# A margin behind planned landings for prologue products, and another tie-breaking number, in a transformer block on one core

## The chip, the cores and the metric

The kernel runs on one core of one Trainium2 chip. The metric is the device time in microseconds of one execution, from runs of the same inputs; the profile is one further execution taken with the hardware profiler. Engines are named as in the profile: PE is TensorE, ACT is ScalarE, DVE is VectorE, POOL is GpSimd, SP is the engine that issues all DMAs here. A tile of tokens is 128 tokens; the sequence has 2048 tokens, so 16 tiles.

## The reference

Model width D = 1024, 32 heads of 32, feed-forward width F = 3584, everything in bf16. Two branches read the same normalised input and meet in a gate:

```python
def reference(A_x, A_wqkv, A_wo, B_x, B_w1, B_b1, B_w2, B_b2):
    def _A_ref(x, wqkv, wo):
        B, S, D = x.shape
        H = 32
        Dh = D // H
        qkv = (lambda x, *d: x.transpose(*d))((x @ wqkv).reshape(B, S, 3, H, Dh), 2, 0, 3, 1, 4)
        q, k, v = qkv[0], qkv[1], qkv[2]
        scores = jnp.einsum("bhqd,bhkd->bhqk", q, k) * (Dh ** -0.5)
        p = _softmax(scores, axis=-1)
        o = jnp.einsum("bhqk,bhkd->bhqd", p, v)
        return (lambda x, *d: x.transpose(*d))(o, 0, 2, 1, 3).reshape(B, S, D) @ wo
    def _B_ref(x, w1, b1, w2, b2):
        y = _layernorm(x, axis=-1)
        h = _gelu(jnp.einsum("bsd,df->bsf", y, w1) + b1)
        return jnp.einsum("bsf,fd->bsd", h, w2) + b2
    x = A_x
    xn = _layernorm(x, axis=-1)
    s = _A_ref(xn, A_wqkv, A_wo)
    g = _silu(_B_ref(xn, B_w1, B_b1, B_w2, B_b2))
    return x + s * g
```

The softmax takes 32 x 2048 x 2048 exponentials, and the kernel computes all of them on ACT.

## The kernel before

**An order made by a planner.** Every operation of the kernel is first recorded as a planned operation (`_Plan.add`) with an engine, a cost (`occ`), a latency and the operations it depends on. `_Plan.run` then plays the five engines forward in planned time and fixes, for each engine, the order in which its operations are issued. `settle` turns the dependencies into semaphore waits and `emit` writes the instructions. Only the order reaches the chip: a planned time is not kept, and each engine goes through its list in order and waits on semaphores.

**Work.** Heads are taken in 8 groups of 4 (`hg`), queries in 8 blocks of 256 (`qb`), keys in 8 blocks of 256 (`kp`). One unit (line 903) is one head group, one query block and one key block: PE makes the scores (8 matmuls, line 919), ACT takes two exponentials of 128x1024 each from PSUM (line 928), and later PE multiplies them with V (line 632). There are 512 such score groups and 1024 exponentials. DVE adds exponentials up for the softmax sums (lines 945, 959, 1329, 1332). The products of the feed-forward branch, the projections of Q, K and V for later head groups, and at the end the output projection, are "dense" work that fills PE between score groups.

**PE's choice.** `pe_step` (line 246) picks PE's next operation in planned time. Score groups come from `s_queue` in a fixed order and have precedence when they are ready or would be delayed (lines 256 and 349). Products of exponentials with V come from `pv_queue`. Dense work comes from named queues in `self.dense`: among them `pro` (the first K and Q blocks of head group 0), `q0` (its later Q blocks), `v0` (its V, in quarters of four tiles), `proj`, `mlp`, `w2`, `wo`. Only the head of each queue is a candidate, `next_dense` (line 219) sorts the heads by position, and an item that has begun is gone through to its end, with score groups between its matmuls. Dense and value items share two PSUM banks, 6 and 7. When PE has nothing to do for long, it may put in filler matmuls (line 329 on).

**The prologue.** Head group 0 can't start until tokens are normalised and turned, so that the model width lies across the partitions. Tiles 0 to 3 and 5 are turned on PE and evicted by ACT (line 804); tiles 4 and 6 to 15 are normalised by DVE into `gw` (line 816) and turned by a DMA from `gw` to `xnT` (line 820). The planner gives such a DMA 1300 ns on SP, 262144 bytes at 300 bytes per ns and for most tiles 1000 ns more (line 821). The products of the prologue read `xnT`: K block n (`k_item`, line 762) and Q block n (`q_item`, 752) tiles 2n and 2n+1, a Q pair of blocks (`qk_item`, 740) and a V quarter m (`v_half`, 726) tiles 4m to 4m+3. A V quarter has 32 matmuls, eight for each tile in order, evicted by DVE at line 736; a K block from the second on has 8 matmuls and is evicted at line 771, a Q block at 758, a Q pair at 748. An item becomes a candidate when its first matmul's operands are there in planned time; for a later tile of a V quarter nothing is asked.

In the score order (`order0`, line 1243) the scores that first need K block 5 are the 15th group, K block 6 the 17th, K block 7 the 19th.

**Tie-breaking numbers.** `nz` (line 83) makes a number between -1 and 1 from a seed, which belongs to a stretch of 30,000 ns of planned time (`plan.seeds`, `plan.seg`), and the operation's index. With seed 0 it is 0. It shifts the positions of `proj`, `mlp`, `w2` and `wo` items (by up to `amp` = 4, line 230), the priorities of DVE operations (by up to `jit` = 0.1, line 158) and the choice of the exponential after which an item of values may begin (line 272). Only the third stretch, 60 to 90 us of planned time, has a seed other than 0.

Of the kernel before, what the change touches and what calls it, by code (L numbers as in the profile page):

```python
# [32 lines left out]
class _Plan:  # L33
# [59 lines left out]
    def run(self):  # L93
# [86 lines left out]
        def bank_for():  # L180
            best = None
            for b in (6, 7):
                if owner[b] is not None and owner[b].k < len(owner[b].chunks):
                    continue
                r = 0.0
                for x in bank_free[b]:
                    if x.start is None:
                        break
                    r = max(r, x.fin)
                else:  # L190
                    if best is None or r < best[0]:
                        best = (r, b)
            return best
# [25 lines left out]
        def next_dense(t):  # L219
            out = []  # L220
            busy = any(owner[b] is not None and owner[b].mode == "v" and (owner[b].evacs[-1].fin or INF) > t for b in (6, 7))
            if not busy and S["pv"] < len(self.pv_queue):
                busy = self.pv_queue[S["pv"]].soon.start is not None
            for n in self.dense:
                q, h = self.dense[n], heads[n]
                if h < len(q) and q[h].hold <= S["s"]:
                    if q[h].due < S["s"] + self.lead:
                        out.append((q[h].due - 1e6, n, q[h]))
                        continue
                    amp = self.amp if n in ("proj", "mlp", "w2", "wo") else 0.0  # L230
                    out.append((q[h].pos - (self.w2b if n == "w2" and busy else 0.0) + amp * self.nz(t, q[h].chunks[0].idx), n, q[h]))
            out.sort(key=lambda x: x[0])
            return out
# [12 lines left out]
        def pe_step(t):  # L246
# [19 lines left out]
            if S["pvo"] is not None:  # L266
                it = S["pvo"]
                vo = it.chunks[it.k]
            elif S["pv"] < len(self.pv_queue):
                it = self.pv_queue[S["pv"]]  # L270
# [16 lines left out]
            if S["do"] is not None:  # L287
                it = S["do"]
                do = it.chunks[it.k]
                if do.left == 0:  # L290
                    d_at = do.ready
                else:
                    do = None
            else:
                bf = bank_for()
                for pos, n, it in next_dense(t):
                    o = it.chunks[0]
                    if it.need is not None and it.need.k < len(it.need.chunks):
                        continue
                    if o.left or (it.bank is None and (bf is None or (held and it.due >= S["s"] + self.lead))) or (it.evacs and not it.heirs and it.evacs[0].left > 1):  # L300
                        continue
                    if n == "w2" and not all(d.start is not None for c in it.chunks for d in c.deps if d.eng == "DVE"):
                        continue
                    if n == "wo" and not all(d.start is not None for d in it.chunks[-1].deps if d.eng != "PE"):
                        continue
                    r = o.ready if it.bank is not None else max(bf[0], o.ready)
                    if r < d_at:
                        do, dopen, d_at = o, (it, None if it.bank is not None else bf[1], n), r
                    if d_at <= t:
                        break  # L310
            v_ok, d_ok = v_at <= t, d_at <= t
            use = None
            it = dopen[0] if dopen else S["do"]
# [13 lines left out]
            if use is None:  # L327
# [5 lines left out]
                if bf is not None and bf[0] <= t and S["s"] < len(self.s_queue):  # L333
                    cw = 430.0 if t < 4800.0 else 220.0
                    wide = t < 4900.0 and nxt > t + cw + 200
                    n, w = (1, 4) if wide else (1, 1) if t < 6000.0 else (2, 1) if t < 10000.0 else (1, 2)
# [16 lines left out]
            if use == "v":  # L353
# [4 lines left out]
                it = S["pvo"]  # L358
# [3 lines left out]
            else:  # L362
# [5 lines left out]
                it = S["do"]  # L368
# [8 lines left out]
        while ev:  # L377
            t, ei = heapq.heappop(ev)
            e = ENGS[ei]
            if t < tf[e]:  # L380
                continue
            while ev and ev[0] == (t, ei):
                heapq.heappop(ev)
            if e == "PE":
                pe_step(t)
                continue
            o = pick(e, t)
            if o is not None:
                commit(o, t)
                if e == "ACT":  # L390
                    S["dry"] = tf[e]
                    for x in pend[e]:
                        if x.prio == 0:
                            S["dry"] += x.occ
                    for x in soon[e]:
                        if x[2].prio == 0:
                            S["dry"] += x[2].occ
            elif soon[e]:
                wake(max(t, soon[e][0][0]), e)
# [71 lines left out]
def bass_recurrent_scan__mha_block__mixer_channel_mlp__prompt_kernel(  # L471
# [24 lines left out]
    plan.pat1, plan.pat2, plan.guard = 3000.0, 900.0, 660.0  # L496
    add = plan.add
    plan.seeds = (
        0, 0, 235064808, 0, 0, 0, 0, 0, 0, 0, 0, 0, 0, 0, 0, 0, 0, 0, 0, 0, 0, 0, 0, 0, 0, 0, 0, 0, 0,
        0, 0, 0, 0, 0, 0, 0, 0)  # L500
    plan.seg, plan.amp, plan.jit = 30000, 4, 0.1

    with ExitStack() as st:
# [870 lines left out]
        for w in range(HG):  # L1374
            if 0 < w < HG - 1:
                proj(w + 1, w)
            if w == HG - 1:
# [6 lines left out]
                v0 = V[:, 1].rearrange("p t n -> p (t n)")  # L1384
# [14 lines left out]
            for qb in range(NQB):  # L1399
# [45 lines left out]
                for t2 in range(2):  # L1445
# [16 lines left out]
                    for nh in range(2):  # L1462
                        late = qb >= NQB - 2
                        fin = qb == NQB - 1
                        it = _Item("wo", 64 * 7 + 8 * qb + 4 * t2 + 2 * nh)
# [140 lines left out]
```

## Time and profile before

| what | value |
|---|---|
| median of 3 runs | 1027.97 us (1027.73 to 1028.23) |
| the profiled execution's own time | 1027.79 us |
| its span, first to last instruction | 1026.0 us |
| granted PE clock | 1.000 |
| exponentials of 128x1024 in PSUM | 1024, of which 988 into the P tiles by line 928: 918.9 us busy |
| DMA | 167.76 MB, mean 164 GB/s |
| tiles turned by DMA | 11, from issue to landing 2.7 / 2.9 / 4.4 us (least, median, most) |
| PE busy from 30 to 60 us | 27.74 of 30 us |
| PE busy from 60 to 90, from 90 to 120 us | 28.68, 29.95 of 30 us |

The table is read from the top: the profiled execution lies within the three runs, and 1.79 us of its time lie around the span. Times in views of the trace count from the span's first instruction. Busy time is the union of instruction times on an engine. In the timeline an instruction's start may lie a little inside the one before it, so the pace of a row of equal instructions is read from the starts of two pieces, not from the durations.

### The profile page before, as it was taken

How to read it: one execution, taken by the hardware profiler on the slowest of the kernel's cores; microseconds unless marked ns; L12 is line 12 of the kernel's file. 1: busy time of each engine (PE TensorE's matmuls, PEld its weight loads, DVE VectorE, ACT ScalarE, POOL GpSimd, SP SyncE). 2: the span in 40 equal slices, each digit the busy share in tenths (PEclk: the TensorE clock that was granted, in tenths of full speed). 3: DMA queues.
4: the chain of work that ended last, by engine and by line, in shares of the span. 5: the costliest groups of instructions: out<-in, count | busy, mean ns of one | idle time of the engine just before them, and what ended most of it. 6: DMA issues, size and time to landing. Idle time of an engine off the chain costs nothing.

```text
span 1026.0 us, 31917 instructions
## 1 busy us (share of the span) xinstructions
PE 993.4 (97%) x14227; PEld 632.5 (62%) x14294; DVE 953.4 (93%) x1364; ACT 1015.5 (99%) x1080; POOL 15.1 (1%) x23
## 2 busy tenths in 40 slices
PE   8899999999999999999999999999999999999997
PEld 6556665776666566656665676666666656564444
DVE  8999999999999998998999999998999889978987
ACT  8999999999999999999999999999999999999997
POOL 2200000000000000000000000000000000000000
PEclk9999999999999999999999999999999999999999
DMA  8558842766675767446456676566457753783331
GB/s 232 123 140 224 215 130 72 200 186 177 177 199 139 200 172 194 138 109 180 131 158 176 172 219 172 141 185 173 119 146 189 213 153 97 245 250 114 124 94 64
DMA packets 315761, 167.76 MB, mean 164 GB/s; under 512 B 54248, under 2 KB 303592, under 8 KB 315624
## 3 DMA queue, kind: packets, MB, share of 16 engines
q1 hardware_dynamic: 315624, 165.72, 57.8%
q8 instruction: 112, 1.84, 0.7%
q14 instruction: 25, 0.20, 0.1%
HBM read 146.55 MB, written 12.06 MB: 155 GB/s over the span
## 4 chain that ended last, share of the span: by engine, by line
ACT 92%; DVE 4%; PE 2%; DMA 1%; issue 0%; POOL 0%; SPq 0%
ACT P L928 84%; ACT ut L1146 5%; ACT P L1277 1%; PE ps L637 1%; ACT ut L1177 1%; DVE stats L856 1%; DMA xnT<-gw 1%; DVE PA L945 1%; DVE PR L959 1%; ACT w2r L928 1%; DVE gw L816 1%; DMA hT<-in_A_x_dram 0%; ACT gw L1177 0%; PE ps L919 0%; POOL lnp L865 0%
## 5 line engine op out<-in xcount | busy, mean ns | idle before, releaser
L928 ACT ACTIVATE P<-ps 128x1024 bf16<-128x1024 f32 x988 | 918.9, 1242 | 0.7 <-PE ps L919 0.7
L945 DVE TENSOR_TENSOR PA<-P 128x2048 bf16<-128x2048 bf16 x173 | 210.0, 1216 | 27.8 <-ACT P L928 27.3
L637 PE MATMUL ps<-yT,w1r 128*128 128x256 bf16 x1792 | 227.1, 273 | 1.1 <-DVE QKT L748 0.7
L637 PE MATMUL ps<-w2r,hT 128*128 128x256 bf16 x1792 | 222.9, 273 | 1.8 <-DVE V L722 1.1
L919 PE MATMUL ps<-QKT 32*128 32x256 bf16 x4032 | 200.2, 273 | 14.2 <-ACT P L928 11.4
L959 DVE TENSOR_TENSOR PR<-PR,PA 128x2048 bf16<-128x2048 bf16 x173 | 209.2, 1212 | 1.3
L637 PEld LDWEIGHTS ps<-yT,w1r 128*128 128x128 bf16 x1792 | 163.9, 98 | 53.4 <-issue 27.7
L637 PEld LDWEIGHTS ps<-w2r,hT 128*128 128x128 bf16 x1792 | 163.2, 98 | 51.4 <-issue 30.6
L919 PEld LDWEIGHTS ps<-QKT 32*128 32x128 bf16 x4032 | 59.8, 92 | 140.5 <-ACT P L928 135.4
L632 PE MATMUL ps<-P,V 128*32 128x256 bf16 (+1 forms) x4080 | 137.4, 272 | 0.0
L637 PE MATMUL ps<-xnT,wqk 128*128 128x512 bf16 (+2 forms) x534 | 119.3, 352 | 4.4 <-DMA xnT<-gw 1.0
L632 PEld LDWEIGHTS ps<-P,V 128*32 128x32 bf16 x4080 | 95.5, 96 | 32.3 <-issue 23.2
L637 PE MATMUL ps<-wv,xnT 128*128 128x256 bf16 (+2 forms) x704 | 87.4, 264 | 1.4 <-DMA xnT<-gw 1.4
L637 PEld LDWEIGHTS ps<-xnT,wqk 128*128 128x128 bf16 x584 | 49.5, 98 | 52.4 <-issue 15.8
L1115 DVE TENSOR_TENSOR hT<-ps,b1T 128x512 bf16<-128x512 f32 x112 | 76.7, 685 | 3.1 <-PE ps L637 2.5
L945 DVE TENSOR_TENSOR PR<-P 128x2048 bf16<-128x2048 bf16 x60 | 72.9, 1215 | 0.5 <-ACT P L928 0.5
L637 PEld LDWEIGHTS ps<-wv,xnT 128*128 128x128 bf16 x704 | 56.1, 98 | 22.9 <-issue 9.9
L1146 ACT ACTIVATE ut<-ut 128x3072 bf16<-128x3072 bf16 (+2 forms) x27 | 59.5, 2206 | 0.0
L748 DVE CAST QKT<-ps 128x512 bf16<-128x512 f32 x58 | 39.6, 683 | 1.5 <-PE ps L637 1.1
L1014 DVE STREAM_TRANSPOSE nt<-ps 128x256 f32<-128x256 f32 x63 | 28.0, 444 | 11.7 <-PE ps L632 11.5
L1140 DVE TENSOR_TENSOR ut<-hT 128x2048 bf16<-128x2048 bf16 (+1 forms) x37 | 35.2, 956 | 0.1
L1149 DVE TENSOR_TENSOR hT<-ut,hT 128x2048 bf16<-128x2048 bf16 (+1 forms) x37 | 35.1, 954 | 0.0
(121 smaller groups left out, 576.5 us busy)
## 6 DMA issues: line engine op xcount, KB each, us to landing
w1r<-in_B_w_dram SPq DMA_DIRECT2D x112, 512.0 KB, 4.3
w2r<-in_B_w_dram SPq DMA_DIRECT2D x128, 256.0 KB, 3.8
w2r<-in_B_w_dram SPq DMA_DIRECT2D x128, 192.0 KB, 3.7
yst<-in_A_x_dram SPq DMA_DIRECT2D x18, 256.0 KB, 4.6
wqk<-in_A_wqkv_dram SPq DMA_DIRECT2D x16, 256.0 KB, 3.5
g_scratch<-gw SPq DMA_DIRECT2D x32, 128.0 KB, 3.2
hT<-in_A_x_dram SPq DMA_DIRECT2D x14, 256.0 KB, 3.8
o_scratch<-ot SPq DMA_DIRECT2D x56, 64.0 KB, 3.2
```

Of the source, the lines that this page charges most:

```text
L632: ins = e.matmul(dst(j), lhsT=lhsT(j), rhs=rhs(j), start=start, stop=stop, tile_position=(0, 32 * j), skip_group_check=True)
L637: return e.matmul(dst, lhsT=lhsT, rhs=rhs, start=start, stop=stop, skip_group_check=True)
L748: dve(lambda e: e.tensor_copy(QKT[sl][:, which, tq * 512:(tq + 1) * 512], bank(it.bank)), c_ps(512), [], [(nm, sl, 2 * tq), (nm, sl, 2 * t ...
L919: ins = e.matmul(bank(b0[j], kk * 256, (kk + 1) * 256), lhsT=QKT[sl][32 * j:32 * j + 32, 1, kb * 128:(kb + 1) * 128], rhs=QKT[sl][32 * j:3 ...
L928: x = act(lambda e, h=h: e.activation(Pt[pi][:, 2 * h:2 * h + 2].rearrange("p j k q -> p (j k q)"), ps[:, pr[h] * 1024:(pr[h] + 1) * 1024] ...
L945: return dve(lambda e: e.tensor_tensor(dst[:].rearrange("p u j q -> p (u j) q"), src[:].rearrange("p u j k q -> p (u j) k q")[:, :, 0, :], ...
L959: return dve(lambda e: e.tensor_tensor(fl3(pr), fl3(pr), fl3(PA[i]), op=ALU.add), c_b16(2048), [("PA", i), tok], [tok], 3.2)
L1014: dve(lambda e: e.transpose(nt_t[:], bank(pv.bank, 256, 512)), c_ps(256) + 120, [], [("nt",)], prio, pv)
L1115: w1_ev[p] = dve(lambda e: e.tensor_tensor(hT[:, hs], bank(it.bank).rearrange("p (k t) -> p k t", k=2), b1T[:, 2 * pi:2 * pi + 2].unsqueez ...
L1140: dve(lambda e, u_=u_, x_=x_: e.tensor_tensor(u_, x_, x_, op=ALU.mult), c_b16(n), hs_, [("ut", ui)], gp)
L1146: act(lambda e: e.activation(ua, ua, ACT.Tanh, scale=GC), c_acts(run * 512), uts, uts, ga)
L1149: dve(lambda e, u_=u_, x_=x_: e.tensor_tensor(x_, u_, x_, op=ALU.mult), c_b16(n), [("ut", ui)] + hs_, hs_, gp)
```

## The change

A new condition in `pe_step`'s search for dense work: after 30 us of planned time, an item of `pro`, `q0` or `v0` is passed over as long as any of its matmuls reads something that a DMA brings which either has not been planned yet or whose planned landing plus 1600 ns lies later than the matmul's own place, taken as now plus 55 ns for each matmul ahead of it in the item. (Both branches of the written choice by position are 1600.) The seed of the third stretch is another number. Nothing else differs; the costs that the planner reckons with are the same.

```diff
                     if o.left or (it.bank is None and (bf is None or (held and it.due >= S["s"] + self.lead))) or (it.evacs and not it.heirs and it.evacs[0].left > 1):
+                        continue
+                    if n in ("pro", "q0", "v0") and t > 30e3 and any(d.eng == "SP" and (d.start is None or d.fin + (1600.0 if it.pos < 0.2 else 1600.0) > t + 55.0 * i)
+                                         for i, c in enumerate(it.chunks) for d in c.deps):
                         continue
...
     plan.seeds = (
-        0, 0, 235064808, 0, 0, 0, 0, 0, 0, 0, 0, 0, 0, 0, 0, 0, 0, 0, 0, 0, 0, 0, 0, 0, 0, 0, 0, 0, 0,
+        0, 0, 234953942, 0, 0, 0, 0, 0, 0, 0, 0, 0, 0, 0, 0, 0, 0, 0, 0, 0, 0, 0, 0, 0, 0, 0, 0, 0, 0,
```

## The prediction

> **What bounds the kernel.** First the page's head and the waits of ACT, then how busy each engine is over the long middle.
>
> ```profile
> span 1026.0 us, 31917 instructions
> PE 993.4 (97%) x14227; PEld 632.5 (62%) x14294; DVE 953.4 (93%) x1364; ACT 1015.5 (99%) x1080; POOL 15.1 (1%) x23
> ...
> ACT PR L1515 <- PE ps L637: 2.9, 1, 2.9
> ACT PA L842 <- DMA hT<-in_A_x_dram: 2.4, 2, 2.0
> ACT L684 <- PEq L1591: 0.7, 1, 0.7
> ACT P L928 <- PE ps L919: 0.7, 1, 0.7
> ACT xnT L804 <- PE ps L800: 0.3, 1, 0.3
> ...
> 120.00:1000.00 880.00, 861.67 (x12004) 546.58 (x12055) 825.51 (x1127) 880.00 (x930) 0.00 (x0) 1.00 0.58 164
> ```
>
> ACT is the bound: 1015.5 of 1026.0 us busy, all 880 us of the middle without a gap. The waits list all its idle time but the end: 2.4 + 0.7 + 0.3 before the exponentials flow, 2.9 at the last product, and one wait of 0.7 us for scores (line 919). The rest, 1026.0 - 1015.5 - 7.0 = 3.5 us, lies behind ACT's last instruction. So the change can only gain from that one 0.7, from the tail, or from exponentials that follow each other more slowly than they could.
>
> The timeline around 34 us shows the wait, and the chain of waits its cause:
>
> ```profile
> 32.75 0.90 PE L637 MATMUL ps<-wv,xnT 128*128 128x128 bf16 x13
> 33.14 1.97 ACT L928 ACTIVATE hT<-ps 128x1024 bf16<-128x1024 f32 x2
> 35.05 0.40 PE L637 MATMUL ps<-wv,xnT 128*128 128x128 bf16 x4 [1.40 <-DMA xnT<-gw]
> 35.38 0.40 PE L919 MATMUL ps<-QKT 32*128 32x256 bf16 x8
> 35.82 1.02 ACT L928 ACTIVATE P<-ps 128x1024 bf16<-128x1024 f32 x1 [0.71 <-PE ps L919]
> 36.14 0.69 DVE L736 CAST V<-ps 128x512 bf16<-128x512 f32 x1 [1.26 <-PE ps L637]
> ...
> 30.64 4.36 DMA xnT<-gw
> 35.00 0.05 issue
> 35.05 0.40 PE ps L637 x4
> 35.44 0.33 PE ps L919 x8
> ```
>
> This is V quarter 2 (tiles 8 to 11). Its first 24 matmuls run (11 from 31.71, 13 from 32.75), then it stands 1.40 us for tile 11, whose turning DMA was issued at 30.64 and landed at 35.00. A score group stands behind it in PE's order: it comes at 35.38, and ACT, done at 35.11, idles 0.71 us. The planner reckons for this DMA 1300 + 262144/300 + 1000 ns = 3.17 us from issue to landing (lines 820 and 821); it took 4.36, so 1.19 over.
>
> **The change, part by part.**
>
> *What V quarter 2 is held for.* With the condition a quarter's matmul 24 may be placed no earlier than 1.60 us behind the planned landing. Planned landing is 1.19 before the real one, so 0.41 us of cover is left at this tile, apart from the lag between planned and real clock, which adds to both. The quarter is therefore not begun at 31.71. What else is a candidate then: K block 5 reads tiles 10 and 11 from its first matmul and is held longer than the quarter; the first Q pair of `q0` comes behind Q block 3, which reads tiles 6 and 7 (landed before 27) and is free. So Q block 3 moves ahead of the quarter: 8 matmuls, about 0.83 us (an equal K block: "31.05 0.83 x6" and two before it). It takes some of the time that was a wait, and the 12th score group no longer stands behind tile 11: ACT gets it by 35.11. Gain: 0.71 us.
>
> *What follows the wait.* DVE's eviction at 36.14 had waited 1.26 us in DVE's order, and behind it stand K block 5's eviction and the normalisation of tiles 14 and 15, whose DMAs were issued at 38.31 and 39.58. Without the wait these come up to 1.26 us earlier. Exponentials follow each other every 0.917 us where nothing is in the way (start 984.08 to 1004.25, 22 of them). Read from starts, two from 33.14 to 35.82 took 0.85 too long, four from 35.82 to 39.61 took 0.12, six from 41.44 to 47.09 took 0.15: 1.12 us in all. The second and third may be echoes of the late tile (the score group at 46.63 follows a PE wait for a V eviction) or may come back with the new order. Bounds of the gain in the prologue: 0 and 1.12; I take 0.71, what the waits name.
>
> *Time that the condition holds PE empty.* From 30 to 60 us PE was busy 27.74 of 30, so 2.26 us were idle, 1.40 of them this wait. Held items leave PE idle instead. Between the 11th and the 12th score group lie 35.11 - 32.75 = 2.4 us, Q block 3 fills 0.83: up to 1.5 us of idle in place of 1.40. That is about even, so no work is pushed behind 60 us in sum. If cover were gone it would cost: PE has 1.32 us free from 60 to 90, and 0.05 from 90 to 120. Fillers: PE was busy without a gap from 28 to 32 us, above the share of 0.6 under which they are put in, so 0; at most one pair, 0.3 us by the three of 0.50 at 21.70, ahead of a score group that has 0.4 to spare.
>
> *K blocks 6 and 7, V quarter 3, Q pairs.* These are held too. Their order among themselves has no free item to change it, so they only come later in relation to the score groups. Cost 0 while the K blocks are in time; the price if not is the first rival.
>
> *The seed.* It adds and removes no instruction; it shifts choices of DVE, of dense items and of value items between 60 and 90 us of planned time, and everything after is planned anew from there. Cover: ACT's unbroken row. PE waits from 90 to 1000 us show what such a row takes without a gap:
>
> ```profile
> PE ps L637 <- DVE V L722: 1.1, 2, 0.7
> PE ps L637 <- DVE QKT L748: 1.0, 2, 0.7
> PE ps L637 <- DMA w2r<-in_B_w_dram: 0.2, 1, 0.2
> ```
>
> PE stood up to 0.7 us and ACT lost nothing; 1.40 us cost 0.71, so some 0.69 us is absorbed each time. I take 0. Bounds: a tail better by 0.5 (of its 2.9 us wait), and new waits of 0.71 each as below. No DMA is added; SP's order may shift with DVE's.
>
> *Sum.* 1027.79 (the profiled execution) - 0.71 = 1027.08. The median of the runs is 0.18 higher, so 1027.26: I say 1027.3.
>
> *A rule against the change.* Row: granted clock is 1.00 in the stage from 34 to 36 us although PE was busy only 0.95 of 2.00 there. The Trainium skill ("TensorE: Matmul & The Clock Gate", Part 1: The HAM clock gate) says that PE falls back to half clock after an idle window of about 3.4 us; this case's trace agrees as far as 1.40 us of idle did not do it, and no run here shows a longer one. It is a rival below.
>
> **Rivals.**
>
> 1. *A held K block is late (slower than before).* K block 6 reads tiles 12 and 13 and must be evicted before the 17th score group, at 44.43. Before, its eviction ran 42.02 to 42.43: 2.00 us to spare, and without the wait ACT is up to 0.85 earlier, so the group is wanted at 43.58. Tile 13's DMA was the first of three issued from 35.66; planned landing and margin are 3.17 + 1.60 = 4.77 behind, 40.43. From there 8 matmuls (two of 0.61) and a score group (0.40) end at 42.05, DVE's eviction takes 0.41 and may stand behind one add of 1.21: 43.67, late by 0.1. So it decides from about 40.4 on: one more such add ahead costs 1.21. Then 1027.26 + 1.21 = 1028.5; with K block 7 late by as much, 1029.7. For: DVE has no gap from 42 to 48 us. Against: eviction of a K block has DVE's first priority (-1, line 772), and tile 13's own path isn't later.
> 2. *The new order has waits of its own after 60 us.* Each landing that is 1.40 us late costs 0.71. Four of them give 1027.26 + 2.84 = 1030.1, from which on it is slower by over 0.2%. For: PE has only 18.3 us free in the 880 of the middle. Against: before there was not one, with the same costs reckoned.
> 3. *It doesn't do what it says.* Landings beyond the margin, or quarter 2 placed so that the score group still stands behind tile 11: the 0.71 stays, 1028.0. For: 1.19 of the 1.60 is already used up at this tile. Against: Q block 3's 0.83 alone is more than the 0.71.
> 4. *PE's clock drops* in the held time, the rule above: at half clock a stage like 36 to 42 us, with 5.95 of 6 us of PE work, would take 6 us more: 1033.2. Against: the granted clock is 1.00 throughout.
>
> **How the numbers follow.** Forecast 0.58 (its own range 1026.6 to 1028.0), rival 1 0.14, rival 2 0.15, rival 3 0.11, rival 4 0.02. The range starts at 1027.97 - 1.12 - 0.5 = 1026.4, rounded; its top, 1029.8, takes in rival 1 with both K blocks and the mild end of rival 2. A measurement of this kernel tells about 0.2%, 2.06 us, from no change: bounds 1025.9 and 1030.0. Faster than that needs the whole 1.12 and nearly 1 us of the tail: 0.03. Slower: most of rival 2 and rival 4 and a little of rival 1, 0.16. Within: 0.81.
>
> **What would show it.** PE's order the same up to about 31.7 us, then Q block 3 (128x256 on `wqk`) ahead of V quarter 2. No wait of PE for `xnT<-gw` behind 30 us, no wait of ACT for line 919, starts 0.917 apart, DVE's eviction at line 736 without 1.26 us of wait, DMAs of tiles 14 and 15 about a microsecond earlier. ACT from 120 to 1000 us busy 880.00. The prediction is wrong if ACT waits anywhere between 36 and 1019 us, or if its tail differs by over 0.5 us.

## The result, and the profile after

| | before | changed |
|---|---|---|
| median, 22 runs each | 1027.94 us | 1026.70 us |
| profiled execution, its span | 1027.79, 1026.0 us | 1026.64, 1024.9 us |

The ratio of changed to before is 0.9988, with a 95% interval of 0.9983 to 0.9994: 1.24 us faster. The interval leaves out 1, but the change is smaller than the 0.2% below which the prediction speaks of no change. One of the 22 runs of before took 1574.57 us and is left out of the ratio. The page's head, ACT's waits and the long middle, of the changed kernel:

```profile
span 1024.9 us, 31991 instructions
PE 1000.4 (98%) x14294; PEld 632.0 (62%) x14294; DVE 953.6 (93%) x1364; ACT 1015.3 (99%) x1080; POOL 13.6 (1%) x23
...
ACT PR L1518 <- PE ps L640: 2.9, 1, 2.9
ACT PA L845 <- DMA hT<-in_A_x_dram: 2.0, 1, 2.0
ACT L687 <- PEq L1594: 0.7, 1, 0.7
ACT xnT L807 <- PE ps L803: 0.3, 1, 0.3
...
120.00:1000.00 880.00, 869.84 (x12053) 547.89 (x12046) 824.92 (x1127) 879.90 (x929) 0.00 (x0) 1.00 0.58 164
```

All lines of the kernel behind the new condition are three further down: line 922 is 919 of before, 931 is 928, 640 is 637. ACT's busy time is the same to 0.2 us, and its wait for scores is gone. PE's busy time seems to grow by 7 us, but no matmul was added: before, 14227 matmuls were recorded beside 14294 weight loads, after, 14294 beside 14294. Some records of before are missing, and PE's busy time there is too low by them.

The timeline of the place where the wait was (start, duration, what, and in brackets the idle time ahead of it):

```profile
30.48 1.48 PE L640 MATMUL ps<-xnT,wqk 128*128 128x256 bf16 x12
31.98 0.40 PE L922 MATMUL ps<-QKT 32*128 32x256 bf16 x8
32.31 0.39 PE L640 MATMUL ps<-xnT,wqk 128*128 128x256 bf16 x2
33.82 0.40 PE L922 MATMUL ps<-QKT 32*128 32x256 bf16 x8 [1.11 <-ACT hT L931]
34.15 1.57 PE L640 MATMUL ps<-wv,xnT 128*128 128x128 bf16 x25
35.65 0.40 PE L922 MATMUL ps<-QKT 32*128 32x256 bf16 x8
36.88 0.68 DVE L739 CAST V<-ps 128x512 bf16<-128x512 f32 x1
```

Q block 3 (the `wqk` matmuls behind the K block's) now runs where quarter 2 began. The 12th score group is the next in the order and waits only for ACT, which is what a score group should wait for; quarter 2 stands behind it and finds tile 11 landed. PE still idles 1.11 us, at a place where it costs nothing. The chain of waits shows what that does to ACT:

```profile
29.18 3.67 ACT P L931 x4
32.85 1.83 ACT hT L931 x2
34.68 3.67 ACT P L931 x4
38.35 1.83 ACT hT L931 x2
40.18 5.50 ACT w1r L931 x6
```

From 29.18 to 45.68 the chain is nothing but exponentials, 18 of them at 0.917 us; before, DMA, PE and DVE were links of it between 28 and 47 us.

The ends of the same exponential in the two traces, one by one, account for the whole difference of these two executions. An exponential is called late by what its end lies over 0.917 us behind the end of the one ahead of it. By 28.7 us the changed kernel is 0.40 us ahead, where the two orders are still the same: inputs landed earlier in that execution (0.4 us less waiting for x in ACT's list). The three late exponentials of before, 0.82, 0.12 and 0.14 us, and crumbs of 0.04, bring it to 1.53 by 50 us, and so it stays until 885 us. There it loses 0.39 at three exponentials between 888 and 917 us, where PE waits for loads of `w2r`, the tile for the second weights of the feed-forward branch. 1.14 remain, 1.1 in the span. The 0.40 at the start belongs to the execution, not to the change.

### The profile page after: what moved, and what is told of

Read it like the earlier page. It is cut to its first block, busy times and chain, and to the rows that moved or that the text cites. A ratio compares the mean times of both kernels' runs of the same rounds, so it can differ in the third digit from the quotient of the medians.

```text
span 1024.9 us, 31991 instructions
## 1 busy us (share of the span) xinstructions
PE 1000.4 (98%) x14294; PEld 632.0 (62%) x14294; DVE 953.6 (93%) x1364; ACT 1015.3 (99%) x1080; POOL 13.6 (1%) x23
## 4 chain that ended last, share of the span: by engine, by line
ACT 91%; PE 4%; DVE 2%; DMA 2%; issue 0%; SPq 0%; POOL 0%
ACT P L931 82%; ACT ut L1149 5%; PE ps L640 3%; DMA w2r<-in_B_w_dram 1%; ACT P L1280 1%; ACT ut L1180 1%; PE ps L922 1%; PE ps L635 1%; DVE PA L948 1%; DVE PR L962 1%; ACT w2r L931 1%; ACT w1r L931 1%; DMA hT<-in_A_x_dram 0%; ACT hT L931 0%; ACT gw L1180 0%
## 5 line engine op out<-in xcount | busy, mean ns | idle before, releaser
L640 PE MATMUL ps<-xnT,wqk 128*128 128x512 bf16 (+2 forms) x584 | 131.9, 354 | 0.9 <-DMA xnT<-gw 0.5
L751 DVE CAST QKT<-ps 128x512 bf16<-128x512 f32 x58 | 39.7, 684 | 2.0 <-PE ps L640 1.7
L1152 DVE TENSOR_TENSOR hT<-ut,hT 128x2048 bf16<-128x2048 bf16 (+1 forms) x37 | 35.1, 952 | 0.0
```

The lines of the kernel that those rows point to most:

```text
L640: return e.matmul(dst, lhsT=lhsT, rhs=rhs, start=start, stop=stop, skip_group_check=True)
L751: dve(lambda e: e.tensor_copy(QKT[sl][:, which, tq * 512:(tq + 1) * 512], bank(it.bank)), c_ps(512), [], [(nm, sl, 2 * tq), (nm, sl, 2 * t ...
L1152: dve(lambda e, u_=u_, x_=x_: e.tensor_tensor(x_, u_, x_, op=ALU.mult), c_b16(n), [("ut", ui)] + hs_, hs_, gp)
```

## The experiments

In what follows the new condition is called the hold, and the time behind the last exponential the tail. Each ratio is against runs of the kernel before that were taken beside the experiment; their medians were 1027.74 to 1028.01 us.

The order that a kernel's planner arrives at can be compared with that of before. By the traces, PE's weight loads (none of their records is missing) come in the same order up to 31.6 us and again from 311 us to the end; ACT's instructions differ from 96 to 282 us only, by where tanh stands among the exponentials.

**Each part alone.** The hold with the old seed:

```diff
-        0, 0, 234953942, 0,
+        0, 0, 235064808, 0,
```

> The hold of prologue items with the seed of before. Theory (the hold makes the gain, the seed only steers the later order): ACT has no wait for line 922 behind 30 us and its exponentials from 28 to 60 us follow each other every 0.917 us, as in the changed kernel. If the seed is otherwise neutral, 1026.7 us. But the order that this pair gives, as the plan in the kernel has it, leaves ACT 0.54 us idle near 516 us and the last product 3.24 us later behind the last exponential than the 2.99 planned before: with that 1026.7 + 4.2 = 1030.9 us. Rival (the seed makes the gain): the 0.7 us wait near 35 us is still there and the time is 1027.9 or more with no change of the tail.

Measured: 1032.21 us, ratio 1.0038 (1.0027 to 1.0050). And the new seed without the three lines of the condition:

> The new seed without the hold. Theory: PE's order up to 60 us is that of before, so the 1.4 us wait of PE for tile 11 and the 0.7 us wait of ACT near 35 us are there, and the later order is a poor one: planned ACT idle of 0.54 us near 516 us and a tail 3.24 us longer, so 1027.9 + 3.8 = 1031.7 to 1032.2 us. Rival (the seed makes the gain): 1026.7 us. Rival (seeds do nothing): 1027.9 us.

Measured: 1033.06 us, ratio 1.0050 (1.0037 to 1.0062). ACT's waits with the hold alone, then with the seed alone, and for the latter PE at tile 11:

```profile
ACT PR L1518 <- PE ps L640: 6.0, 1, 6.0
ACT P L931 <- PE ps L922: 1.4, 2, 0.9
```

```profile
ACT PR L1515 <- PE ps L637: 6.0, 1, 6.0
ACT P L928 <- PE ps L919: 1.0, 2, 0.6
...
32.78 0.90 PE L637 MATMUL ps<-wv,xnT 128*128 128x128 bf16 x13
34.97 0.40 PE L637 MATMUL ps<-wv,xnT 128*128 128x128 bf16 x4 [1.30 <-DMA xnT<-gw]
```

Both parts alone make the kernel slower, for the same reason: the order between 60 us and the end is another one, its last product comes 3.1 us later behind the exponentials (6.0 instead of 2.9), and an exponential at 517 us is 0.54 late. In the prologue the two differ as the theory has it. The hold alone has not one late exponential between 31 and 517 us, the seed alone has those of before (0.72, 0.12 and 0.13). The rival that the seed makes the gain has fallen. Both kernels came out up to 1.4 us over what was expected, though for the hold the two terms named come to 3.8 us and not to the 4.2 that were added. Part of it lies behind the last product: from the last exponential to the end of the span both traces take 11.2 us and the one of before 6.8, so the whole tail is 4.4 longer, where the 3.24 of the plan went to the product alone. In the profile of the hold alone another 1.03 is one exponential at 895 us, behind a PE wait of 1.1 us for w2r.

**Other seeds that keep the short tail**, one for the kernel before (6859424) and one for the changed one (101029822).

> The kernel before with a third seed whose planned order again ends with the short tail (2.99 us planned), no hold. Theory (the hold makes the gain): PE waits 1.3 to 1.4 us for tile 11, the exponentials are late by 0.7 to 0.8, 0.12 and 0.13 us as before: 1027.9 us, 1027.5 to 1028.3. Rival (the gain comes from what a new seed does after 60 us): 1026.7.

Measured: 1028.00 us, ratio 1.0002 (0.9993 to 1.0010). PE waits 1.26 us for tile 11, the exponentials are late by 0.68, 0.12 and 0.13. One more is 1.03 late at 129 us, behind a turning DMA `yT<-yst` that took 5.65 us to land; its order differs from that of before there, and one trace can't tell whether the order or the execution made it late.

> The changed kernel with a third seed whose order ends with the short tail, with the hold. Theory: no late exponential from 28 to 90 us, and at 890 to 920 us a few tenths lost to late w2r landings: 1026.7 us, 1026.3 to 1027.1. Rival (the particular new seed matters): 1027.9.

Measured: 1026.73 us, ratio 0.9993 (0.9984 to 1.0002), an interval that just reaches 1; in its profile no exponential behind 20 us is late, and the span is 1024.2 us. The medians are those of before and of the changed kernel to 0.1 us. With two seeds each, the kernels without the hold are at 1027.9 and 1028.0 us, those with it at 1026.7 and 1026.7: the hold makes the gain, and of the seed only the order matters to which it leads.

**Which part of the hold.** With a margin of 0:

```diff
-... d.fin + (1600.0 if it.pos < 0.2 else 1600.0) > t + 55.0 * i)
+... d.fin + (0.0) > t + 55.0 * i)
```

> The hold with a margin of 0 instead of 1600 ns, so that an item is only passed over while a tile's planned landing lies behind its matmul; seed of the third stretch chosen so that the order behind 310 us is that of before and after. Theory (moving Q block 3 ahead is what matters): the score group is placed ahead of tile 11's matmuls, PE may still wait up to 0.5 us for the tile, ACT idles 0 to 0.2: 1026.7 to 1027.0 us. Rival (the 1.6 us are needed, because the landing is 1.2 us later than planned): PE waits about 1 us and ACT 0.7 as before: 1027.9 us.

Measured: 1027.04 us, ratio 0.9990 (0.9982 to 0.9998). PE around tile 11:

```profile
32.85 1.28 PE L640 MATMUL ps<-wv,xnT 128*128 128x128 bf16 x20
34.08 0.40 PE L922 MATMUL ps<-QKT 32*128 32x256 bf16 x8
34.41 0.40 PE L640 MATMUL ps<-wv,xnT 128*128 128x128 bf16 x4
35.23 0.62 PE L640 MATMUL ps<-wv,xnT 128*128 128x128 bf16 x8 [0.41 <-DMA xnT<-gw]
```

Refusing an item whose tile has not landed in the plan is enough to move Q block 3 ahead and to bring the score group in front of tile 11's matmuls. PE still stands 0.41 us for the tile, and exponentials are late by 0.21, 0.12 and 0.07 between 37 and 48 us. So the 1.6 us are worth those 0.4 in the trace (another exponential, at 896 us, is 0.37 late behind w2r); the medians, 0.3 apart with overlapping runs, don't settle that.

With the hold for quarter 2 alone (`n == "v0" and it is self.dense["v0"][2] and t > 30e3`):

> The hold for V quarter 2 alone, with a seed that gives the short tail. K block 5, which reads tiles 10 and 11 from its first matmul, is then free at their planned landing and comes between Q block 3 and quarter 2, with four of its matmuls ahead of the 12th score group. Theory (what has to stay behind the landing is every matmul of tile 11 ahead of a score group): PE waits for tile 11 about 1 us at K block 5, the score group stands behind it, ACT loses 0.6 to 0.9 near 35 us: 1027.5 to 1028.0 us. Rival (only the quarter matters): 1026.7.

Measured: 1028.57 us, ratio 1.0010 (1.0001 to 1.0019); PE at the same place:

```profile
32.61 0.39 PE L640 MATMUL ps<-xnT,wqk 128*128 128x256 bf16 x2
34.89 0.49 PE L640 MATMUL ps<-xnT,wqk 128*128 128x256 bf16 x3 [1.89 <-DVE gw L819]
35.31 0.40 PE L922 MATMUL ps<-QKT 32*128 32x256 bf16 x8
```

The name behind the arrow is that of the tile's preparation, long done; the last thing to come was tile 11, landed at 34.80. K block 5 has taken quarter 2's place ahead of the score group and waits 1.89 us, and the exponential is 0.94 late. The stall belongs to whatever reads tile 11 in front of a score group, not to the quarter. One more exponential is 0.38 late at 356 us. That the median is 0.6 over the expected range isn't explained by this profile, whose own time is 1027.85 and whose granted clock is 1.00; the list of the runs points to the clock. Seven of the twelve have a mean granted clock of 0.998 and took 1028.54 to 1031.19 us, the five with 0.999 or 1.000 took 1026.84 to 1028.29. Half clock for 3.4 us lowers the mean over 1026 us by 0.0017, and the next experiment shows such a stretch.

With the hold for everything but quarter 2 (`it is not self.dense["v0"][2]` added to the condition):

> The hold for all prologue items but V quarter 2. Theory (the wait stood in quarter 2): PE waits 1.4 us for tile 11 and ACT 0.7 as before; no seed of 150 gave this order the short tail, the best is planned 0.95 us longer: 1027.9 + 0.95 = 1028.9 us. Rival (the K blocks and later items behind their margin make the gain): the waits of 0.12 and 0.15 and part of the 0.7 vanish, 1027.7 us with that tail.

Measured: 1030.57 us, ratio 1.0022 (1.0014 to 1.0031). The profiled execution was the longest of the twelve, 1033.56, and shows something else. First PE, then the stages (us; busy time and count of PE, PEld, DVE, ACT, POOL; granted PE clock; DMA share and GB/s):

```profile
35.53 0.40 PE L640 MATMUL ps<-wv,xnT 128*128 128x128 bf16 x4 [1.82 <-DMA xnT<-gw]
35.86 0.40 PE L922 MATMUL ps<-QKT 32*128 32x256 bf16 x8
36.19 0.53 PE L640 MATMUL ps<-wv,xnT 128*128 128x128 bf16 x4
36.51 2.34 PE L640 MATMUL ps<-xnT,wqk 128*128 128x256 bf16 x10
38.78 0.61 PE L922 MATMUL ps<-QKT 32*128 32x256 bf16 x8
...
34.00:36.00 2.00, 0.47 (x12) 0.34 (x12) 0.84 (x3) 1.18 (x2) 0.00 (x0) 1.00 0.27 61
36.00:38.00 2.00, 2.00 (x19) 1.39 (x12) 0.77 (x2) 1.69 (x2) 0.40 (x1) 0.58 0.90 201
38.00:39.00 1.00, 1.00 (x12) 0.44 (x10) 0.54 (x2) 0.25 (x1) 0.76 (x3) 0.50 0.00 0
39.00:40.00 1.00, 1.00 (x13) 0.53 (x6) 0.80 (x2) 0.55 (x1) 0.91 (x2) 0.63 0.00 0
40.00:41.00 1.00, 1.00 (x8) 0.45 (x5) 0.63 (x2) 1.00 (x2) 1.00 (x1) 1.00 0.50 115
```

The wait is there, 1.82 us in this execution, and the first exponential is 1.24 late. After it the granted clock falls to 0.50 until shortly before 40 us. Ten matmuls that took 1.34 us before take 2.34, a score group 0.61 instead of 0.40, and the next exponentials are late by 1.31 and 0.30. (Another 2.0 us of this execution are two late exponentials near 917 us, behind w2r, and its tail is 1.8 us longer than before, where 0.95 was planned.) So the wait for tile 11 can cost more than 0.71 us: here it was 0.4 us longer, and the clock fell behind it. The lists of runs fit that it falls less often with the hold. Of the 79 runs of before that were taken beside the experiments nine have a mean clock of 0.997 or 0.998, at 1028.96 to 1030.93 us; of the 55 of the changed kernel, its other seed and the last version below one has, at 1029.07. Where in those runs the clock fell isn't on record.

**The margin doubled**, with the best seed found for it:

> The hold with twice the margin, 3200 ns, best seed found. It prices the first rival of the prediction, a K block held too long. Theory: no wait for tile 11, but K blocks are late: the plan itself leaves ACT 0.38 us idle at 40, 0.22 at 44 and 1.72 at 49 us, each ahead of a score group that needs a new K block; on the chip 2.3 us in all less what the planner's earlier landings take away or add: 1026.7 + 2.3 = 1029.0 us, 1028.5 to 1029.8. Rival (a larger margin costs nothing): 1026.7.

Measured: 1029.05 us, ratio 1.0015 (1.0006 to 1.0023). ACT:

```profile
40.18 5.83 ACT L931 ACTIVATE w1r<-ps 128x1024 bf16<-128x1024 f32 x6 [0.22 <-PE ps L922]
45.90 1.95 ACT L931 ACTIVATE w2r<-ps 128x1024 bf16<-128x1024 f32 x2
49.46 3.77 ACT L931 ACTIVATE w2r<-ps 128x1024 bf16<-128x1024 f32 x4 [1.62 <-PE ps L922]
```

No exponential is late near 35 us, but three are at 40, 44 and 49 us, by 0.33, 0.22 and 1.72 us: held K blocks, as planned to within 0.05. A fourth, at 357 us, is 0.70 late behind a PE wait for a DVE eviction, in a stretch where the order is another one; so that the median came out as expected is in part luck.

**What is lost near 900 us.** The changed kernel once more, and a version with some loads held back:

```diff
         def load_o(hc):
+            held = [owed[1][HELD[hc]][0]] if hc in HELD and owed else []
...
-                [("o_d", hc, q) for q in range(NQB)], [("OTr", hc)], extra=dead, rate=390.0, lat=3700.0)
+                [("o_d", hc, q) for q in range(NQB)], [("OTr", hc)], extra=dead + held, rate=390.0, lat=3700.0)
```

where `HELD = {3: 1, 4: 3, 5: 5}`, with one more seed in the 33rd stretch.

> The changed kernel once more. Theory (what it loses near 888 to 917 us comes from w2r loads that land late in this execution, not from its order, which is that of before there): no late exponential from 28 to 90 us again, and between 0 and 0.4 us lost at 888 to 917 us, another amount than the 0.39 of the first profile; 1026.7 us. Rival (the loss belongs to the new order): 0.39 us again at the same exponentials.

> The changed kernel with three of the five 512 KB loads into xnT that are issued together near 878 us held back, one after another, behind exponentials of the last query block of head group 6, and a seed in another late stretch that keeps the short tail. Theory (w2r loads land late because they share the DMA engines with these): w2r loads issued from 878 to 890 us land 2 us sooner, no late exponential there, 1026.4 us, a gain of 0 to 0.4 on the changed kernel, at the edge of what runs can tell. Rival (later loads only move the crowd to 895 to 910 us): the same 0 to 0.4 lost there, 1026.7.

Measured: 1027.07 us, ratio 0.9990 (0.9981 to 0.9999), and 1027.00, ratio 0.9991 (0.9982 to 1.0000). PE's waits for w2r from 870 to 930 us in the first profile of the changed kernel, in its second and with the loads held back:

```profile
PE ps L640 <- DMA w2r<-in_B_w_dram: 1.2, 3, 0.7
```

```profile
PE ps L640 <- DMA w2r<-in_B_w_dram: 2.1, 4, 1.0
```

```profile
PE ps L638 <- DMA w2r<-in_B_w_dram: 0.2, 1, 0.2
```

In the second profile no exponential is late between 29 and 890 us. The same order lost 0.39 us behind 885 us in one execution and 1.20 in another, and the kernel before 0: it is when the w2r loads land, 8 to 10 us after issue beside 512 KB loads, and not the order. In the kernel before the slowest of them took 9.9 us and no exponential was late, so a few tenths decide. A quieter start of that crowd took the wait away in one execution, but the other-seed version of the changed kernel lost nothing there either, without it, and the medians are equal. That it helps isn't shown; no version was found that is faster than the changed kernel beyond what runs can tell.

## Why the prediction was right, and where its sizes were off

*The bound and the place.* Right: ACT is the bound, and what there was to gain was the wait behind tile 11 and what follows from it. The order was the same up to there, Q block 3 moved ahead of quarter 2, PE has no wait for `xnT` behind 30 us, the V eviction no longer waits, and the DMA of tile 14 was issued 1.8 us earlier (at 36.53 by the trace, 38.31 before), 0.6 of it because tile 10's already was.

*"I take 0.71, what the waits name."* The mis-sized term. The bound of 1.12 from the starts was the answer: all three late exponentials vanish, 1.08 us by their ends. An idle time in the waits list leaves out what the late exponential loses beyond its gap (0.71 listed, 0.82 late), and the other two were echoes: they are in every run with PE's wait for tile 11 in its quarter at full clock (before, its other seed, the seed alone), and in none of the five profiles with the whole hold at 1.6 us. For the last of them the chain of waits of before shows the way, from the eviction of quarter 2 through an unbroken row of DVE work to that of quarter 3, for which PE waits ahead of a score group:

```profile
36.14 0.69 DVE V L736
...
44.79 0.61 DVE V L736
45.41 0.27 issue
45.68 1.03 PE ps L637 x4
46.70 0.36 PE ps L919 x8
47.09 5.62 ACT w2r L928 x6
```

For the one of 0.12 only the runs speak. The medians' 1.24 (0.6 to 1.8 by the interval) can't tell 0.71 from 1.12; the traces can. That the two profiled executions lie 1.15 apart, near the 1.12, is luck in part: the changed one wins 0.40 at the start and loses 0.39 near 900 us.

*"Time that the condition holds PE empty"* was about even, as said: 1.11 us of idle in place of 1.40 ahead of the 12th score group, without new fillers; from 30 to 60 us PE was busy for 27.45 us, before for 27.74.

*The seed: "I take 0."* Right for the pair, wrong as a term of its own. ACT's unbroken row was named as its cover, but the row is a property of one order, and any change at 31 us makes the planner choose anew for the rest of the kernel. With the old seed the hold costs 4.2 us, and the new seed without it 5.1. Two parts that seemed independent were one.

*Rival 1, a late K block,* is real and lies at a larger margin: 0 at 1.6 us, 2.3 at 3.2. *Rival 2, waits of the new order,* came only as w2r landings of 0.4 to 1.2 us, in a stretch whose order had not changed. By its own sign (no wait of ACT from 36 to 1019 us, 880.00 us busy from 120 to 1000) the prediction missed there by a little: 879.90 in the first profile, 879.28 in the second. The 18.3 us of free PE named for this rival were too many, because of the missing records: the changed kernel's trace, with all of them, has 10.2. *Rival 3:* the margin was less needed than argued; 0 already moves the score group. *Rival 4, the clock:* not in the profile of the changed kernel, 1.00 to its last instruction. But a fall of the clock happens in this kernel, behind the kind of stall that the change removes, and after a shorter wait than the rule in the prediction asks for. The price of 6 us was too high: about 3.4 us of half clock cost ACT 1.6, the wait's echoes included.

*The planned landing.* The prediction took the 1.19 us by which tile 11 came later than planned as given and asked for no cause. The last section has a reading that fits every trace.

## What to carry to other kernels

In an order made by a planner a stall comes from an operation placed by an optimistic landing in front of the one that feeds the bound; refusing such a placement costs nothing as long as something else is free, and costs a late operand beyond that. Any early change of a greedy order redraws everything behind it, so compare it with a tie-break that brings the later order back, or the price of the redraw is taken for that of the change. Where one engine runs without a gap, the ends of its instructions one by one tell tenths of a microsecond apart and where they were lost, while the medians of 22 runs leave an interval 1.2 us wide; but they tell it of one execution.

## What was not expected of the hardware

The granted clock fell to 0.50 after a PE wait of 1.82 us, with PE busy 0.47 of 2.00 us in that stage, and stayed there from about 36.3 to 39.7 us. The wait of 1.89 us in the run with the hold for quarter 2 alone left it at 1.00. The Trainium skill ("TensorE: Matmul & The Clock Gate", Part 1: The HAM clock gate) has the fall after an idle window of about 3.4 us, on windows that run freely: the time at half clock agrees with such a window, the length of the wait doesn't. The two runs together suggest that it is where the wait falls, and the traces bear that out. In each of the twelve the granted clock is on record in pieces, and all but the last are whole multiples of 3.413 us long (30.72, 3.41 and 989.87 us where it fell), so the stretches can be counted back from one change. In the run with the fall the stretch from 32.91 to 36.32 us, at whose end the clock fell, holds the whole wait, and PE was busy for 1.59 of its 3.41 us. With the hold for quarter 2 alone a border at 33.30 cuts the wait, and the stretch behind it has 1.83 us of busy PE. A limit can't be read from this: at the end of the kernel before a stretch with 1.52 us busy (1020.51 to 1023.92) was not followed by a fall.

The DMA that turns tile 11 took 4.32 to 4.97 us from issue to landing in the twelve traces, that of tile 10, issued 1.3 us ahead of it, 2.7, at equal size. Being second of a pair isn't the reason: tile 13, second of the next pair, took 2.9. Two views of the kernel before, for the DMAs of tiles 10 and 11 from 30.7 to 35.1 us and for those of tiles 12 and 13 from 35.7 to 38.6, show a difference (GB/s in 40 slices; queues with packets, MB and share; the issues with median us to landing):

```profile
GB/s 291 289 296 279 296 293 270 99 5 0 9 144 279 293 291 284 291 293 293 329 26 0 0 0 0 0 0 0 0 0 0 0 0 0 0 0 0 0 0 0
q8 instruction: 1, 0.02, 1.4%
xnT<-gw SPq DMA_TRANSPOSE x2, 3.5
```

```profile
q1 hardware_dynamic: 2021, 0.50, 76.9%
xnT<-gw SPq DMA_TRANSPOSE x2, 2.8
```

Tile 11's data had moved by 33.0 us, but it landed at 35.00. In between lies one packet of 16384 bytes of the queue of kind "instruction", from 32.85 to 33.82 us, and two 4-byte packets of the tile's own queue end right behind it, by 33.84. So it is in all twelve traces: the packet begins 2.2 to 3.0 us behind tile 11's issue and takes 0.9 to 1.5 us, and the last small packets end 0.01 to 0.02 us behind it; tiles 10 and 13 have none in any of them. Such a packet also lies in the DMAs of tile 6, which took 3.8 to 4.8 us. It doesn't always delay: at 437 us of the kernel before with its other seed a turning DMA of `yT` with one took 3.2 us, like those without. That this packet makes tile 11 late is the reading that fits; no run moved it. For tiles 4, 6 and 7 the planner has longer times of their own (line 821), for tile 11 it has not; giving it one is a rival to the margin that was not tried.
